# The order of optional blocks at the end of a routed expert layer

## Chip, cores and metric

The kernel runs on one core of one Trainium2 chip. The metric is device time in microseconds, as the median of several runs. All data are float32.

## The reference

A mixing layer (the real part of a Fourier transform along the sequence and along the features) feeds a layer of eight experts. Each of the 19968 rows goes to the one expert with the highest logit.

```
X = np.fft.fft(x, axis=1)              # x: (8, 2496, 256)
X = np.fft.fft(X, axis=2)
x = X.real.reshape(19968, 256)

logits = x @ w_gate                    # (19968, 8)
expert_idx = np.argmax(logits, axis=1)
# ... gate_w: softmax probability of the chosen expert
# ... rows sorted by expert; lo, hi bound the rows of expert e
for e in range(E):
    h = np.maximum(x_sorted[lo:hi] @ w1[e], 0.0)   # 256 -> 1024
    y_sorted[lo:hi] = h @ w2[e]                    # 1024 -> 256
y = gate_w[:, None] * y_sorted[inv_perm]
```

How many rows each expert gets is known only when the kernel runs.

## The kernel before

The eight batches are mixed one after the other. Their rows are scattered into a buffer `Xs` in HBM, grouped by expert. Between the mixing steps, and then alone, the kernel works through a list of blocks. A block has 512, 256 or 128 rows of one expert. Which expert and which rows is read from a table that the kernel computes on the chip; the number of blocks and their order are fixed when the program is built.

The last round has five blocks of 512 rows, seven of 256 rows (numbered 0 to 6), and 21 small blocks of 128 rows (numbered 0 to 20). The first 14 small blocks exist whatever the routing is. Small blocks 14 to 20 are optional: they take up the partly filled ends of the experts, and a routing may need fewer than all of them.

```
    # rounds(), last batch
    k = full(done, BLK)                                   # 7 blocks of BLK = 256 rows
    now.append((BLK, k, False))
    now.append((REST, (NT - used + E * (REST - 1)) // REST, True))   # 21 blocks of REST = 128

SURE = -(-(NT - sum(size * k for now in rounds() for size, k, last in now if not last)) // REST)   # 14

def in_order():
    todo = []
    for b, now in enumerate(rounds()):
        parts = [[(b, size, last, i) for i in range(k)] for size, k, last in now]
        if b == B - 1:
            few, many = parts[-2:]
            sure, more = many[:SURE], many[SURE:]
            k = len(few)
            rest = []
            for i in range(k):
                rest += few[i:i + 1] + sure[len(sure) * i // k:len(sure) * (i + 1) // k][:1]
                rest += more[len(more) * i // k:len(more) * (i + 1) // k]
                rest += sure[len(sure) * i // k:len(sure) * (i + 1) // k][1:]
            parts = parts[:-2] + [rest]
        todo += sum(parts, [])
    return todo
```

A block loads its rows and the two weight matrices of its expert, 1 MiB each. Rows and weights have three buffers each, so a block reuses the buffers of the third block before it. The loads of up to three blocks, the current one included, are asked for in the order of the list, all on one queue:

```
    def fetch_rows(b, size, tab, i):
        ...
        xb = bp.tile([128, BIG // 128, W], F32, tag="xb", name="xb", bufs=3)
        taken(nc.sync.dma_start(out=xb..., in_=Xs[ds(row, size)]...), b)          # L528

    def fetch_weights(tab, i):
        ...
        w1_sb = bp.tile([128, 2, F], F32, tag="w1", name="w1_sb", bufs=3)
        nc.sync.dma_start(out=w1_sb[:], in_=w1[ds(ev, 1)]...)                      # L535
        w2_sb = bp.tile([128, FC, D], F32, tag="w2", name="w2_sb", bufs=3)
        nc.sync.dma_start(out=w2_sb[:], in_=w2[ds(ev, 1)]...)                      # L537
```

Products of an optional block stand in a branch. If the block isn't used, a short product of a bfloat16 tile of ones takes their place. Everything else of an unused block still runs: loads, transposes, the activations, and the scatter of its rows, whose indices lie outside the output.

```
        @contextmanager
        def needed(last, at, o):
            if not last or at < SURE:
                yield
                return
            ...                       # used = number of small blocks that this routing has
            with tc.If(used > at) as has:
                yield
            with has.Else():
                mm(o[:], ones[0:1], bc(ones[0:1], 1, o[0:1].free_size() // 128))
```

A small block, in the order in which TensorE sees it. `turn` is the transpose of the next block's rows; it stands between the two products.

```
            for f in range(FC // m):                         # two rounds for a small block
                ph = pse.tile([128, m, size], F32, tag="ac"[f % 2], name="ph")
                with needed(last, at, ph):
                    ...  mm(ph[:, j], w1_sb[...], xT[:, c, 0:size], c == 0, c == 1)
                ...      # relu into hT, on ScalarE or VectorE
            ...
            for i in range(n):                               # n = 1 for a small block
                xT = next(turned, xT)                        # transposes pt, L576, L577
                py = pse.tile([128, D], F32, tag="bd"[i % 2], name="py")
                with needed(last, at, py):
                    ...  mm(py[:], hT[...], w2_sb[:, f], f == 0, f == FC - 1)
                y = bp.tile([128, D], F32, tag="y", name="y", bufs=6)
                act.activation(y[:], py[:], ACTF.Copy, scale=xb[:, i, D + 1:D + 2])   # L830
                put_row(out, ro[:, i:i + 1], y[:], NT - 1, "out")
```

The blocks of 256 rows use a scheme of seven products in place of eight, in both layers (products a, b, c, d and e in the profile). It needs sums and differences of the weights, which VectorE makes while the block before runs:

```
    class Left:
        def __init__(self, w1_sb):
            ws = bp.tile([128, 3, F // 2], F32, tag="ws", name="ws", bufs=2)
            ...
        def step(self):
            ...
                vec.tensor_tensor(o, p, q, op=op)            # L556: ws <- w_sb, four operations
```

Of the kernel before, what the change touches and what calls it, by code (L numbers as in the profile page):

```python
# [131 lines left out]
def rounds():  # L132

    want = [((256, 2), (128, 4)), ((256, 4),)] + [((512, B),)] * (B - 2)
    plan, used = [], 0

    def full(done, size):
        return max(0, -(-(done - used - E * (size - 1)) // size))  # L140

    for b in range(B):
        done = (b + 1) * S
        now = []
        for size, most in want[b]:
            k = min(full(done, size), most)
            if k:
                now.append((size, k, False))
            used += size * k
        if b == B - 1:  # L150
            k = full(done, BLK)
            used += BLK * k
            now.append((BLK, k, False))
            now.append((REST, (NT - used + E * (REST - 1)) // REST, True))
        plan.append(now)
    return plan
# [6 lines left out]
# [7 lines that stand above are left out]
            few, many = parts[-2:]  # L170
            sure, more = many[:SURE], many[SURE:]
            k = len(few)
            rest = []
            for i in range(k):
                rest += few[i:i + 1] + sure[len(sure) * i // k:len(sure) * (i + 1) // k][:1]
                rest += more[len(more) * i // k:len(more) * (i + 1) // k]
                rest += sure[len(sure) * i // k:len(sure) * (i + 1) // k][1:]
            parts = parts[:-2] + [rest]
        todo += sum(parts, [])
    return todo  # L180

# [33 lines left out]
def kernel(ctx: ExitStack, tc, x, w_gate, w1, w2, out):  # L215
# [687 lines left out]

    tabs, whole = {}, set()
    todo = in_order()
    for _ in first(0):
        pass
# [108 lines left out]
```

## Time and profile before

| | |
|---|---|
| median of three runs | 1347.98 us (1344.14 to 1348.62) |
| span of the profiled execution | 1337.0 us |
| mean granted TensorE clock | 0.979 |
| HBM traffic over the span | 187 GB/s |
| loads of weights | 132, of 1024 KB each |
| scaled tiles y of 128 rows | 129 |

A row of the page's groups has the source line, the engine and the operation, then what it writes and reads, and how often. After the first bar stand busy time in us and mean length in ns, after the second the idle time ahead of it and what ended most of that. In the chain of waits a row has the start in us, the length in us and what it was. PE is TensorE, DVE is VectorE, ACT is ScalarE, POOL is GpSimd, SPq is the sequencer that issues the loads.

A row of a window has the stretch in us and its length, then busy time of PE, PEld (weight loads into the array), DVE, ACT and POOL, each with its number of instructions, then the granted clock, the busy share of the DMA engines and GB/s.

### The profile page before, as it was taken

What the parts mean: (1) busy time and instruction counts of PE and PEld (TensorE: products, weight loads), DVE (VectorE), ACT (ScalarE), POOL (GpSimd) and SP (SyncE); (2) the same over time, 40 slices, a digit from 0 to 9 for tenths busy, and PEclk for the clock granted to TensorE, in tenths of its full rate; (3) what the DMA queues carried; (4) which work ended last, traced back from release to release, by engine and by line L of the source; (5) the groups of instructions that cost most, each with busy time, mean ns of one, the idle gap of its engine ahead of it and who ended that gap; (6) DMA issues with size and microseconds to landing.
All of it is one profiled execution on the core that took longest, in us unless ns stands there. A gap on an engine that the chain in (4) does not pass through costs nothing.

```text
span 1337.0 us, 20538 instructions
## 1 busy us (share of the span) xinstructions
PE 1272.2 (95%) x7231; PEld 1115.2 (83%) x7231; DVE 706.6 (53%) x1772; ACT 396.2 (30%) x942; POOL 359.8 (27%) x355
## 2 busy tenths in 40 slices
PE   6778997999999999999999999999999999999998
PEld 4667985786688888888888888888889999999887
DVE  4554153243356655565356655467478775444453
ACT  1422131131134332442234333342223232222222
POOL 0335214125211521044111531144354221111111
PEclk9869998999999999999999999999999999999999
DMA  8877867535534832455223742234343237777774
GB/s 248 259 260 275 325 221 248 192 102 161 202 109 155 293 132 99 132 199 198 103 103 119 236 160 103 95 134 141 112 144 148 88 110 288 281 281 276 284 284 173
DMA packets 63107, 249.73 MB, mean 187 GB/s; under 512 B 10057, under 2 KB 24883, under 8 KB 43420
## 3 DMA queue, kind: packets, MB, share of 16 engines
q1 hardware_dynamic: 46231, 203.33, 44.3%
q0 software_dynamic: 15888, 42.14, 8.6%
q10 hardware_dynamic: 885, 2.94, 0.7%
q8 instruction: 59, 0.97, 0.3%
q14 instruction: 44, 0.36, 0.1%
HBM read 194.97 MB, written 54.83 MB: 187 GB/s over the span
## 4 chain that ended last, share of the span: by engine, by line
PE 86%; DMA 4%; DVE 3%; issue 3%; another core or an unknown queue 2%; ACT 1%; POOL 0%; SPq 0%; POOLq 0%; ACTq 0%; DVEq 0%
PE py L220 31%; PE ph L220 10%; PE c L220 10%; PE a L220 9%; PE d L220 6%; PE p L220 6%; PE b L220 5%; PE e L220 4%; PE s L220 3%; PE pt L576 3%; DMA w_sb<-in_moe_w_dram 1%; DMA Td<-t 1%; DMA t<-Td 1%; DMA xq<-in_x_dram 1%
## 5 line engine op out<-in xcount | busy, mean ns | idle before, releaser
L220 PE MATMUL py<-w_sb,hT 128*128 128x256 f32 x2016 | 458.8, 381 | 4.0 <-DVE hT L789 4.0
L220 PEld LDWEIGHTS py<-w_sb,hT 128*128 128x128 f32 x2016 | 375.9, 191 | 52.2 <-DVE hT L789 4.8
L235 POOL DMA_INDIRECT out_dram<-y,ro x163 | 161.9, 993 | 794.0 <-ACT y L830 556.2
L235 POOL DMA_INDIRECT Xs<-rows,pi x160 | 161.9, 1012 | 176.4 <-DVE rows L410 52.3
L220 PE MATMUL ph<-xT,w_sb 128*128 128x128 f32 (+2 forms) x992 | 176.4, 333 | 15.7 <-issue 9.9
L830 ACT ACTIVATE y<-py,xb 128x256 f32<-128x256 f32 x129 | 61.1, 474 | 390.6 <-PE py L220 374.8
L220 PEld LDWEIGHTS ph<-xT,w_sb 128*128 128x128 f32 x992 | 137.7, 195 | 43.8 <-issue 26.9
L220 PE MATMUL a<-xT,w_sb 128*128 128x256 f32 (+1 forms) x512 | 118.3, 358 | 4.3 <-DVE xT L577 4.3
L789 DVE TENSOR_SCALAR hT<-ph 128x512 f32<-128x512 f32 x43 | 29.7, 690 | 172.8 <-issue 77.6
L614 DVE TENSOR_TENSOR u<-p,b 128x512 f32<-128x512 f32 x57 | 39.2, 687 | 138.3 <-PE b L220 96.1
L220 PEld LDWEIGHTS a<-xT,w_sb 128*128 128x128 f32 x512 | 89.6, 192 | 15.1 <-DVE xT L577 5.1
L408 DVE COPY lg<-p 128x16 f32<-128x16 f32 x80 | 13.9, 173 | 128.5 <-ACT zs L405 118.8
L577 DVE TENSOR_SCALAR xT<-pt,table 128x512 f32<-128x512 f32 (+1 forms) x94 | 63.3, 673 | 31.2 <-PE pt L576 31.1
L624 ACT ACTIVATE hT<-a 128x512 f32<-128x512 f32 x57 | 34.0, 597 | 153.8 <-PE a L220 134.1
L220 PE MATMUL s<-xq,w 104*112 104x256 f32 (+2 forms) x208 | 63.3, 428 | 14.8 <-DVE xq L297 11.1
L220 PEld LDWEIGHTS p<-table,t 120*128 120x128 f32 x352 | 55.3, 206 | 11.4 <-issue 4.9
L220 PE MATMUL p<-table,t 120*128 120x120 f32 (+1 forms) x352 | 59.9, 294 | 2.8 <-issue 1.4
L791 ACT ACTIVATE hT<-ph 128x512 f32<-128x512 f32 x55 | 32.8, 597 | 98.9 <-PE ph L220 77.1
L220 PE MATMUL p<-table,zz 128*128 128x145 f32 (+1 forms) x320 | 57.6, 304 | 4.6 <-issue 2.7
L220 PE MATMUL c<-xT,ws 128*128 128x256 f32 (+1 forms) x256 | 59.0, 357 | 2.8 <-DVE hT L620 2.8
L220 PEld LDWEIGHTS s<-xq,w 104*112 104x112 f32 x208 | 39.4, 207 | 25.5 <-DVE xq L297 10.1
L220 PE MATMUL b<-xs,ws 128*128 128x256 f32 (+1 forms) x256 | 59.6, 361 | 0.0
(146 smaller groups left out, 1785.0 us busy)
## 6 DMA issues: line engine op xcount, KB each, us to landing
w_sb<-in_moe_w_dram SPq DMA_DIRECT2D x132, 1024.0 KB
xq<-in_x_dram SPq DMA_DIRECT2D x24, 896.0 KB
xb<-Xs SPq DMA_DIRECT2D x28, 516.0 KB
Td<-t SPq DMA_DIRECT2D x18, 448.0 KB
t<-Td SPq DMA_DIRECT2D x8, 768.0 KB
t<-Td SPq DMA_DIRECT2D x8, 640.0 KB
xb<-Xs SPq DMA_DIRECT2D x13, 258.0 KB
xb<-Xs SPq DMA_DIRECT2D x25, 129.0 KB
```

Source lines behind the costliest of these rows:

```text
L220: nc.tensor.matmul(o, lhsT=lhsT, rhs=rhs, start=start, stop=stop, **kw)
L235: return unordered(pool.indirect_dma_start(out=dst, out_offset=bass.IndirectOffsetOnAxis(ap=idx, axis=0), in_=rows, in_offset=None, bounds ...
L408: vec.tensor_copy(lg[:, k:k + 2], p3[:, NY:NY + 2 * E].rearrange("p (m e) -> p m e", m=2))
L576: nc.tensor.transpose(pt[:, c, t], xb[:, 2 * h + t, c * 128:(c + 1) * 128], ident[:])
L577: vec.tensor_scalar(xT[:, :, 256 * h:256 * h + 128 * n], pt[:].rearrange("p c t k -> p c (t k)"), con["alt"][:], None, op0=ALU.mult)
L614: vec.tensor_tensor(u2[:], p1[:], b[:], op=add)
L624: act.activation(h11, a[:], ACTF.Relu)
L789: vec.tensor_scalar(o, ph[:], 0.0, None, op0=ALU.max)
L791: act.activation(o, ph[:], ACTF.Relu)
L830: act.activation(y[:], py[:], ACTF.Copy, scale=xb[:, i, D + 1:D + 2])
```

## The change

Before, the seven optional small blocks are spread: one behind each 256-block and its first sure small block. Now the first four of them stay among the blocks, each between the two sure small blocks of its 256-block as before, and the other three are put behind everything else. A routing that needs few optional blocks then has the unused ones at the end of the list. Loads, products and branches of each block are untouched.

```
             few, many = parts[-2:]
             sure, more = many[:SURE], many[SURE:]
             k = len(few)
+            end = more[(len(more) + 1) // 2:]
+            more = more[:len(more) - len(end)]
             rest = []
             for i in range(k):
                 rest += few[i:i + 1] + sure[len(sure) * i // k:len(sure) * (i + 1) // k][:1]
-                rest += more[len(more) * i // k:len(more) * (i + 1) // k]
+                rest += more[i:i + 1]
                 rest += sure[len(sure) * i // k:len(sure) * (i + 1) // k][1:]
-            parts = parts[:-2] + [rest]
+            parts = parts[:-2] + [rest + end]
         todo += sum(parts, [])
     return todo
```

The end of the list, with B for a block of 256 rows, s for a sure small block and o for an optional one:

```
before  ... B4 s8 o18 s9  B5 s10 o19 s11  B6 s12 o20 s13
after   ... B4 s8 s9  B5 s10 s11  B6 s12 s13  o18 o19 o20
```

Up to B4 and s8 both lists are the same.

More of the change, by code (lines that the diff above doesn't have):

```diff
@@ L172, in in_order @@
             k = len(few)
+            end = more[(len(more) + 1) // 2:]
+            more = more[:len(more) - len(end)]
             rest = []
@@ L175, in in_order @@
                 rest += few[i:i + 1] + sure[len(sure) * i // k:len(sure) * (i + 1) // k][:1]
-                rest += more[len(more) * i // k:len(more) * (i + 1) // k]
+                rest += more[i:i + 1]
                 rest += sure[len(sure) * i // k:len(sure) * (i + 1) // k][1:]
-            parts = parts[:-2] + [rest]
+            parts = parts[:-2] + [rest + end]
         todo += sum(parts, [])
```

## The prediction

> **What bounds the kernel now.** I read the page first, then the chain of waits and one-microsecond windows for the last 230 us, because the change only moves blocks there. The page:
>
> ```profile
> PE 1272.2 (95%) x7231; PEld 1115.2 (83%) x7231; DVE 706.6 (53%) x1772; ACT 396.2 (30%) x942; POOL 359.8 (27%) x355
> PE 86%; DMA 4%; DVE 3%; issue 3%; another core or an unknown queue 2%; ACT 1%; POOL 0%; SPq 0%; POOLq 0%; ACTq 0%; DVEq 0%
> L220 PE MATMUL py<-w_sb,hT 128*128 128x256 f32 x2016 | 458.8, 381 | 4.0 <-DVE hT L789 4.0
> L830 ACT ACTIVATE y<-py,xb 128x256 f32<-128x256 f32 x129 | 61.1, 474 | 390.6 <-PE py L220 374.8
> ```
>
> TensorE carries 86% of the chain. The last two rows also say how many optional blocks are absent on these inputs: a 128-row tile of py takes 16 records (the chain shows x16 per small block), so 2016 / 16 = 126 tiles were multiplied, yet 129 were scaled into y. Three tiles had no product. Py from the stand-in operand ones runs at 1257.7, 1291.7 and 1323.9 us, so these are small blocks 18, 19 and 20, behind small blocks 8, 10 and 12. They are exactly the three that the change moves.
>
> How the last stage runs when nothing is absent is in the chain, at the first product of 256-blocks 2, 3 and 4 (columns: start, length, what):
>
> ```profile
> 1167.53 0.89 PE a L220 x8
> ...
> 1202.21 0.89 PE a L220 x8
> ...
> 1236.88 0.89 PE a L220 x8
> ```
>
> One 256-block with three present small blocks takes 34.67 us twice running, and all of it is TensorE in the chain. So weights, four pairs of 1 MiB per 34.67 us, don't bound it. From 1236.88 on it is different:
>
> ```profile
> 1253.40 3.47 PE py L220 x16
> 1256.89 0.48 ACT y L830
> 1257.39 0.34 SPq L528
> ...
> 1258.55 7.08 DMA w_sb<-in_moe_w_dram
> 1265.65 0.70 DVE ws L556
> ...
> 1268.27 0.67 DVE xT L577
> 1268.94 0.04 issue
> 1268.99 1.76 PE a L220 x8
> 1270.75 1.71 PE b L220 x8
> 1272.45 1.11 PE d L220 x8
> 1273.56 0.89 PE c L220 x8
> ```
>
> Here small block 8 ends, absent block 18 follows, and 256-block 5 needs the weight buffer that small block 8 has just released (three buffers, so block k uses that of block k-3). The absent block passes in under 2 us, small block 9 in 7.4 us, and the load (7.08 us), the four DVE operations on it and the turn of xT come out later than that. TensorE waits, then also runs at a reduced clock:
>
> ```profile
> 1268.00:1269.00 1.00, 0.01 (x1) 0.01 (x1) 0.97 (x3) 0.00 (x0) 0.52 (x1) 1.00 1.03 421
> 1269.00:1270.00 1.00, 1.00 (x6) 1.00 (x7) 0.93 (x4) 0.00 (x0) 0.00 (x0) 0.69 1.09 459
> 1270.00:1271.00 1.00, 1.00 (x7) 1.00 (x7) 0.96 (x3) 0.22 (x1) 0.00 (x0) 0.50 0.94 387
> ```
>
> (Last three columns: granted clock, DMA share, GB/s.) An absent block therefore costs more than its own few instructions: it is too short to hide the load that it sits in front of.
>
> **What the Trainium skill says.** "Trace Analysis", section Identifying Performance Opportunities, says that the same gap repeating on the engine that should be saturated can mean too few buffers. The trace agrees: the wait appears behind both absent blocks that have a 256-block two places later. "TensorE: Matmul & The Clock Gate", Part 1, says that an idle window of about 3.4 us, free-running, halves the clock. Here the idle stretch is 2.6 us after a nearly idle microsecond at 1258, and 0.50 is granted at 1270; the second such gap, 1.7 us at 1300.4, brought no drop. So direction agrees and the threshold is not settled here. "DMA: Bandwidth & Descriptors", Anatomy of one DMA, gives about 2.0 us plus bytes / 436 GB/s, fitted on another issue path. For the 2.2 MB of rows and weights of a small block that is an estimate of 7.1 us; the trace has 8.9 us, from the issue of the rows at 1316.57 to the last busy DMA window, ending near 1325.45.
>
> **The change, removed part.** The undisturbed length without any optional block is 34.67 minus one small block. In the chain a small block is 3.57 (ph) + 0.22 (pt) + 3.46 (py) = 7.25 us; so 34.67 - 7.25 = 27.42 us. The three groups before, from starts of the first product a:
> - 256-block 4 to 5: 1268.99 - 1236.88 = 32.11, excess 4.69 (about 1.8 for the absent block itself, 2.6 for the wait).
> - 256-block 5 to 6: 1302.06 - 1268.99 = 33.07, excess 5.65 (1.9 from the slow clock on three products of 0.89, 1.8 absent block, 1.7 wait).
> - 256-block 6 to the last y at 1332.14: 30.08. Undisturbed it is 27.42 less 0.22, since no 256-block follows and two transposes fewer are needed: 27.20. Excess 2.88 (1.8 absent block, about 1.0 for late ws operands).
> Sum 13.2 us. After the change the same three buffers suffice: each 256-block takes the buffer of the 256-block before it, which is free two small blocks (14.7 us) ahead, against a load of about 9 us. I expect all 13.2 to go, and the last present y to start at 1332.14 - 13.2 = 1318.9.
>
> **The change, added part.** Before, the span ended 4.9 us after the last y started (1337.0 - 1332.14). Now three absent blocks follow. Their instructions take about 1.8 us each, or 5.4. But absent block 20 loads its rows and both weight matrices although nothing multiplies them, and their buffers are those of small block 13, the last present one. So that load cannot start before its y is scaled. From the same pattern before: y starts, 0.48 later it is done, rows are issued, and 8.9 us later the DMA engines are quiet: 9.4 us. The program ends only when each transfer has landed; for the completion and the closing barrier I take 1.5 us, a choice somewhat below the 2 us that lie between the last busy DMA window (1334 to 1335) and the end at 1337.0 before. That makes 10.9 us. Beside it lies the compute path: rows landed about 2.5 us after y, transposes, the stand-ins of two blocks, y and the scatter: about 7 us to the scatter and 2 to 3 to the end, so 9 to 10, hidden under the load. In the built program the stand-ins wait for no weight transfer; only the multiplied branch does. So the tail grows from 4.9 to 10.9: plus 6.0.
>
> Elsewhere nothing moves: 1671 TensorE instructions are listed for both, and the order before small block 8 is the same. Sum: -13.2 + 6.0 = -7.2 us. 1347.98 - 7.2 = 1340.8 us, or 0.5%.
>
> **Rivals.** (1) *The tail takes it all back.* If only the stand-ins' 3 x 1.8 = 5.4 us leave the middle and the waits remain in another form, -5.4 + 6.0 = +0.6: 1348.6. For it: DMA is 77 to 79% busy in the windows from 1120 to 1280, so the load may simply bind later. Against: the undisturbed groups carry four pairs of weights in 34.67 us, a denser load than three pairs in 27.4, without one wait, and DMA stands at 0 GB/s from 1312 to 1315. (2) *The tail is longer:* the load of absent block 19 is still running when that of 20 begins, and stand-ins might queue behind weights; 14 us of tail would leave -4: 1344. (3) *The tail is hidden further:* if the load finishes at the measured bandwidth peak and the closing is short, about 8.5 us after y, the gain is 9.6: 1338.4. (4) *TensorE, with no gaps, loses clock.* Against it: granted clock 1.00 through 1120 to 1240 us at 100% busy. I give it little.
>
> **Range and chances.** The mechanism spans -10 to +1 around -7.2; the three runs before span 4.5 us (1344.14 to 1348.62), which blurs a median by some 2 us. Together I take 1335.5 to 1346.0. 2% would be 27 us, more than the whole tail and all three waits together, so within 2% is 0.98, and 0.01 each side.
>
> **What would show it.** Right: products a of 256-blocks 4, 5 and 6 are 27.4 us apart, no chain piece of w_sb between them, the clock at 1.00, last y of a present block near 1319, then TensorE almost idle, DMA at about 400 GB/s for 5 to 6 us after it, and the end 11 us after. Wrong in the middle: groups of 29 us or more, with DVE ws still waiting for DMA. Wrong at the end: the last chain pieces are ACT and POOL rather than the weights, or the end comes over 13 us after the last present y.

## The result, and the profile after

The changed kernel takes 1336.3 us (1332.64 to 1337.62) against 1347.07 us (1344.14 to 1348.62) for the one before: ratio 0.9918, 95% interval 0.9892 to 0.9945. Forecast were 1340.8 us and a range of 1335.5 to 1346.0. Measured again in two later sets of runs, the ratio was 0.9948 (0.9933 to 0.9962) and 0.9951 (0.9933 to 0.9969), which is 6.9 and 6.6 us. The forecast gain of 7.2 us lies in both later intervals, and just outside the first, which begins at 7.4 us.

The page of the changed kernel, in the rows that answer to those of before. (The change adds two lines to the source, so L220 is now L222 and L830 is L832.)

```profile
PE 1269.9 (95%) x7231; PEld 1113.9 (83%) x7231; DVE 708.2 (53%) x1772; ACT 396.7 (30%) x942; POOL 359.1 (27%) x355
PE 69%; issue 19%; POOL 3%; DVE 3%; DMA 2%; another core or an unknown queue 2%; ACT 1%; POOLq 0%; ACTq 0%; DVEq 0%; SPq 0%
L222 PE MATMUL py<-w_sb,hT 128*128 128x256 f32 x2016 | 458.5, 381 | 3.9 <-DVE hT L791 3.9
L832 ACT ACTIVATE y<-py,xb 128x256 f32<-128x256 f32 x129 | 61.2, 474 | 396.4 <-PE py L222 381.4
```

The work is the same: equal numbers of instructions, 2016 records of py, 129 tiles y. The second row misleads. TensorE has not fallen from 86% to 69% of what bounds the kernel. The chain of this trace is followed back along GpSimd's own queue, where long stretches are only called issue; in a second trace of the same kernel it stays with TensorE, at 88%. For this kernel the timeline and the windows tell more.

The middle first: 256-block 5 in the timeline of after (start, length, then the instruction; in brackets the idle time ahead of it and what ended that).

```profile
1253.29 0.34 SPq L530 DMA_DIRECT2D xb<-Xs  x1
1254.74 0.05 SPq L537 DMA_DIRECT2D w_sb<-in_moe_w_dram  x1
...
1263.28 0.69 DVE L558 TENSOR_TENSOR ws<-w_sb 128x512 f32<-128x512 f32 x1 [6.03 <-DMA w_sb<-in_moe_w_dram]
...
1265.82 0.74 DVE L579 TENSOR_SCALAR xT<-pt,table 128x512 f32<-128x512 f32 x1
...
1267.05 1.05 PE L222 MATMUL a<-xT,w_sb 128*128 128x128 f32 x8
```

Its load is now asked for when 256-block 4 ends. DVE still waits for it, 6 us long, but TensorE does not: two present small blocks run meanwhile, and product a has no bracket. The reserve is thin. The load lands 10.0 us after its rows were asked for, DVE needs 3.3 us more until xT is ready at 1266.56, and a starts 0.5 us later.

Now the end, first in the timeline of after. The last present block scales its y at 1322.31.

```profile
1322.31 0.47 ACT L832 ACTIVATE y<-py,xb 128x256 f32<-128x256 f32 x1 [4.82 <-PE py L222]
...
1322.81 0.34 SPq L530 DMA_DIRECT2D xb<-Xs  x1
...
1326.56 0.41 PE L578 MATMUL pt<-table,xb 128*128 128x128 f32 x2 [2.41 <-DMA xb<-Xs]
...
1328.83 0.47 ACT L832 ACTIVATE y<-py,xb 128x256 f32<-128x256 f32 x1 [0.46 <-issue]
1329.58 0.97 POOL L237 DMA_INDIRECT out_dram<-y,ro  x1 [0.64 <-ACT y L832]
```

The rows of absent block 20 are asked for 0.50 us after that y starts and let TensorE go on 3.75 us later. Its y starts at 1328.83, its scatter at 1329.58; the end comes 4.9 us after that. In the windows the DMA share and GB/s are the last two columns:

```profile
1324.00:1325.00 1.00, 0.15 (x1) 0.00 (x0) 0.73 (x2) 0.44 (x1) 0.70 (x2) 1.00 0.93 286
...
1330.00:1331.00 1.00, 0.00 (x0) 0.00 (x0) 0.00 (x0) 0.00 (x0) 0.55 (x1) 0.50 0.74 295
1331.00:1332.00 1.00, 0.00 (x0) 0.00 (x0) 0.00 (x0) 0.00 (x0) 0.00 (x0) 0.50 0.07 9
```

So the DMA engines work for the absent blocks until about 1331, with TensorE nearly idle.

Executions differ by 2 to 3 us before 256-block 4 even starts, where both kernels have the same instructions (the changed kernel reached it 2.9 us later in the first pair of traces, 2.1 us in the second). I therefore cut the traces at its first product. What follows is called the stage; a group runs from one 256-block to the next. All numbers below are us, from the starts of product a of 256-blocks 4, 5 and 6 (B4, B5, B6), the last present y, and the end.

| kernel | B4 to B5 | B5 to B6 | B6 to last present y | y to end | sum | ratio to before (interval) |
|---|---|---|---|---|---|---|
| before | 32.27 | 33.07 | 30.08 | 4.86 | 100.28 | 1 |
| before, again | 32.18 | 32.77 | 30.08 | 4.85 | 99.88 | 0.9996 (0.9981 to 1.0011) |
| after | 27.44 | 27.84 | 27.42 | 12.19 | 94.89 | 0.9918 (0.9892 to 0.9945) |
| after, again | 27.44 | 27.43 | 27.48 | 12.69 | 95.04 | 0.9948 (0.9933 to 0.9962) |
| after, third | 27.43 | 27.72 | 27.41 | 12.24 | 94.80 | 0.9951 (0.9933 to 0.9969) |
| without 18, 19, 20 | 27.43 | 27.44 | 27.20 | 4.57 | 86.64 | 0.9898 (0.9882 to 0.9913) |
| optional block ahead of both | 30.80 | 30.96 | 30.02 | 4.85 | 96.63 | 0.9957 (0.9940 to 0.9974) |
| middle, no weights loaded | 31.48 | 32.94 | 30.08 | 4.89 | 99.39 | 1.0017 (0.9999 to 1.0035) |
| middle, loads in a branch | 30.80 | 32.10 | 30.11 | 4.89 | 97.90 | 1.0011 (0.9995 to 1.0026) |
| middle, no weights, asked earlier | 29.49 | 29.49 | 29.25 | 5.00 | 93.23 | 0.9923 (0.9895 to 0.9950) |
| block 20 alone at the end | 32.50 | 33.56 | 29.15 | 5.82 | 101.03 | 0.9979 (0.9959 to 1.0000) |
| end, no weights loaded | 27.43 | 27.44 | 27.41 | 9.52 | 91.80 | 0.9938 (0.9920 to 0.9956) |
| end, loads in a branch | 27.43 | 27.44 | 27.41 | 9.56 | 91.84 | 0.9934 (0.9911 to 0.9957) |
| end, loads in a branch, again | 27.44 | 27.92 | 27.41 | 9.75 | 92.52 | 0.9926 (0.9894 to 0.9957) |

Ratios are to runs of the kernel before on the same chip, whose median was 1347, 1318, 1319 or 1343 us. From the traces the change is worth 5.2 us (three traces of after, mean 94.91, against two of before, mean 100.08): 12.7 won in the middle, 7.5 lost at the end. Each trace is a single execution. In this table trace and timing differ by nearly 6 us in the first measurement of after and by up to 3.8 us in the others, in either direction.

### The profile page after: what moved, and what is told of

Same layout as the page of the kernel before. It is cut to its first block, busy times and chain, and to the rows that moved or that the text cites. A ratio compares the mean times of both kernels' runs of the same rounds, so it can differ in the third digit from the quotient of the medians.

```text
span 1334.5 us, 20538 instructions
## 1 busy us (share of the span) xinstructions
PE 1269.9 (95%) x7231; PEld 1113.9 (83%) x7231; DVE 708.2 (53%) x1772; ACT 396.7 (30%) x942; POOL 359.1 (27%) x355
## 4 chain that ended last, share of the span: by engine, by line
PE 69%; issue 19%; POOL 3%; DVE 3%; DMA 2%; another core or an unknown queue 2%; ACT 1%; POOLq 0%; ACTq 0%; DVEq 0%; SPq 0%
PE py L222 27%; PE p L222 7%; PE c L222 7%; PE a L222 6%; PE ph L222 6%; PE d L222 4%; PE s L222 3%; PE b L222 3%; POOL out_dram L237 3%; PE e L222 3%; PE pt L578 2%; DMA Td<-t 1%; DMA t<-Td 1%; DVE s L775 1%
## 5 line engine op out<-in xcount | busy, mean ns | idle before, releaser
L222 PE MATMUL py<-w_sb,hT 128*128 128x256 f32 x2016 | 458.5, 381 | 3.9 <-DVE hT L791 3.9
L222 PEld LDWEIGHTS py<-w_sb,hT 128*128 128x128 f32 x2016 | 375.6, 191 | 51.9 <-DVE hT L791 4.7
L222 PE MATMUL ph<-xT,w_sb 128*128 128x128 f32 (+2 forms) x992 | 177.5, 335 | 15.8 <-issue 10.4
L832 ACT ACTIVATE y<-py,xb 128x256 f32<-128x256 f32 x129 | 61.2, 474 | 396.4 <-PE py L222 381.4
L222 PEld LDWEIGHTS ph<-xT,w_sb 128*128 128x128 f32 x992 | 138.5, 195 | 44.3 <-issue 29.2
L222 PE MATMUL a<-xT,w_sb 128*128 128x256 f32 (+1 forms) x512 | 117.4, 356 | 0.0
L222 PEld LDWEIGHTS a<-xT,w_sb 128*128 128x128 f32 x512 | 89.3, 190 | 10.1
L222 PE MATMUL s<-xq,w 104*112 104x256 f32 (+2 forms) x208 | 63.3, 429 | 13.6 <-DVE xq L299 11.3
L222 PEld LDWEIGHTS p<-table,t 120*128 120x128 f32 x352 | 55.1, 206 | 11.0 <-issue 3.6
L222 PE MATMUL p<-table,zz 128*128 128x145 f32 (+1 forms) x320 | 57.6, 304 | 5.2 <-issue 2.7
L222 PE MATMUL p<-table,t 120*128 120x120 f32 (+1 forms) x352 | 59.4, 293 | 2.6 <-ACT t L374 1.1
L222 PE MATMUL c<-xT,ws 128*128 128x256 f32 (+1 forms) x256 | 59.0, 357 | 1.2 <-DVE hT L622 0.6
L222 PEld LDWEIGHTS s<-xq,w 104*112 104x112 f32 x208 | 39.4, 207 | 24.3 <-DVE xq L299 10.1
L222 PE MATMUL d<-xT,w_sb 128*128 128x256 f32 (+1 forms) x256 | 58.7, 356 | 0.0
```

Of the source, the lines that this page charges most:

```text
L222: nc.tensor.matmul(o, lhsT=lhsT, rhs=rhs, start=start, stop=stop, **kw)
```

## Experiments

**Both kernels again.** No edit.

> The kernel before once more, unchanged. From the first product of 256-block 4 to the end it took 100.3 us in the first trace. Theory A (the whole gain lies in the last stage): this stage is 100 to 101 us again, and the ratio to before is 1.000. Rival B (the last stage of before is often worse than in its first trace, because the slow clock after the two waits falls differently each time): the stage is 2 to 6 us longer than 100.3 in this trace, which would explain why the runs differ by 11 us and the stage in the traces by only 5.4.

The last stage took 99.88 us and the ratio was 0.9996. Rival B gets no support: in this second trace the stage of before is not worse than in the first.

> The changed kernel once more, unchanged. Theory A: 0.9945 to 0.996 of before (5.4 to 7.4 us less), the stage from 256-block 4 to the end near 94.9 us as in its first trace. Rival C (the program as a whole got another 5 us from the part before 256-block 4, where both have the same instructions): 0.992, and the first product of 256-block 4 earlier than in before by about 5 us.

> The changed kernel a third time, beside the two kernels that it is compared with: 0.993 to 0.996 of before, stage 95 us, tail 12 to 13 us.

Ratios 0.9948 and 0.9951, stages 95.04 and 94.80, as theory A has it, at the upper side of its gain. Rival C (0.992) lies outside both intervals, and product a of 256-block 4 came at 1219.06 in after, against 1216.92 in before on the same chip: no gain hides there. The 0.9918 of the first measurement was not met again.

**Without the three absent blocks.** What do they cost at either place?

```
-            parts = parts[:-2] + [rest + end]
+            parts = parts[:-2] + [rest]
```

> The changed order with optional blocks 18, 19 and 20 left out altogether (this routing has no rows for them; another routing could). It shows what the three cost at either place. Theory A: groups 27.4, 27.8 and 27.3 us as after, the end 4.9 us behind the last y, so the stage takes 87.6 us: 12.7 less than before and 7.3 less than after; ratio to before 0.990. Rival D (the wait in the middle comes from the rate of DMA, not from the absent blocks): groups stay near 29 us or more, ratio above 0.994.

The stage took 86.64 us, within 1 us of the forecast. So the three cost 13.4 us in the middle and 8.3 us at the end. Rival D falls here.

**The optional block ahead of both small blocks.** All 21 are loaded.

```
-                rest += few[i:i + 1] + sure[len(sure) * i // k:len(sure) * (i + 1) // k][:1]
-                rest += more[len(more) * i // k:len(more) * (i + 1) // k]
-                rest += sure[len(sure) * i // k:len(sure) * (i + 1) // k][1:]
+                rest += few[i:i + 1] + more[len(more) * i // k:len(more) * (i + 1) // k]
+                rest += sure[len(sure) * i // k:len(sure) * (i + 1) // k]
```

> Order before, but in each group the optional block stands ahead of both sure small blocks, directly behind the 256-block. All 21 blocks are loaded. The next 256-block then takes the buffer of the optional block, free two whole small blocks (14.7 us) ahead. Theory A (an absent block costs much only because it is the short cover of a 256-block's load): the waits go, only the 1.8 us of each absent block stay: groups of 29.2, 29.2 and 29.0, end 4.9 later, stage 92.3 us, so 8 less than before and 2.6 less than after; ratio 0.994. Rival D (DMA rate): four loads in a group take 32 us or more wherever the absent one stands; stage 100 us, ratio 1.000. Rival E: the second small block behind the absent one now waits for its load (cover 9.2 us), groups of 30.5 to 32, stage 96 us.

Groups of 30.80 and 30.96: neither 29.2 nor 32. (The ratio, 0.9957 with 0.9940 at the lower end, just allows theory A as well; it is the groups that speak against it.) The 256-block's buffer is indeed free early, but so is another. In the timeline of this kernel:

```profile
1233.30 0.34 SPq L534 DMA_DIRECT2D w_sb<-in_moe_w_dram  x1
...
1235.05 0.34 SPq L527 DMA_DIRECT2D xb<-Xs  x1
1236.20 0.71 SPq L534 DMA_DIRECT2D w_sb<-in_moe_w_dram  x1
...
1245.94 0.69 DVE L555 TENSOR_TENSOR ws<-w_sb 128x512 f32<-128x512 f32 x1 [7.78 <-DMA w_sb<-in_moe_w_dram]
...
1249.27 1.16 PE L219 MATMUL a<-xT,w_sb 128*128 128x128 f32 x8 [0.98 <-DVE xT L576]
```

The absent block passes so quickly that two loads are asked for within 3 us. The second, for the 256-block, lands 9.7 us after its issue, and TensorE waits 0.98 us. The windows show 385 to 464 GB/s in every microsecond from 1236 to 1246, so I read this as D in small: not the mean rate of DMA but two loads at once. No run tested that reading alone. Rival E's size was right, but the block that waits is the 256-block.

**In the middle, absent blocks without weights.** Order before; blocks 18 to 20 share the weight tiles of the block ahead of them, so nothing is loaded for them. That leaves out their weights, which this routing doesn't use.

```
+                    if last and at >= MOST - 3:
+                        got.append(shared[0])
+                    else:
                         got.append(fetch_weights(tabs[b, size, last], at))
+                    shared[:] = got[-1:]
```

> Order before, but blocks 18, 19 and 20 load no weights and take no weight buffers: in the program they share those of the block ahead (a routing that used them would get wrong rows; this one doesn't). Rows, stand-ins, activations and scatters stay. Theory A2 (the wait in the middle is the load of the next 256-block made late by the absent block's own load and by the buffer that it turns over): both waits go, each absent block costs its 1.6 to 1.8 us alone. Groups 29.2, 29.2, 29.0, tail 4.9, stage from 256-block 4 to the end 92.3 us against 100 before; ratio 0.994. Rival F (an absent block is itself what holds TensorE up, through its branches and the rows that it loads): groups stay at 31 us or more, ratio 0.998 or above.

Nothing gained: 1.0017, groups of 31.48 and 32.94. Theory A2 falls, at least as it was put, and these are the sizes that rival F named. From the timeline of this kernel:

```profile
1237.58 0.47 ACT L835 ACTIVATE y<-py,xb 128x256 f32<-128x256 f32 x1 [4.80 <-PE py L220]
...
1238.08 0.34 SPq L528 DMA_DIRECT2D xb<-Xs  x1
...
1239.20 0.34 SPq L535 DMA_DIRECT2D w_sb<-in_moe_w_dram  x1
...
1245.55 0.69 DVE L556 TENSOR_TENSOR ws<-w_sb 128x512 f32<-128x512 f32 x1 [6.23 <-DMA w_sb<-in_moe_w_dram]
...
1248.89 1.16 PE L220 MATMUL a<-xT,w_sb 128*128 128x128 f32 x8 [1.82 <-DVE xT L577]
```

By the order in which the buffers turn, the weights of the 256-block had a free one here long before 1239. But they stand on one queue behind its rows, and the rows still rotate through three buffers: their load waits for the y of small block 8 (1237.58, 0.47 long) and is issued at 1238.08. The weights follow 1.1 us later. On this reading a wait on one buffer holds up everything behind it on the queue; the run that asks earlier, below, tests it against rival F.

**In the middle, loads in a branch.** Written to be right for every routing (only this one was run): an absent block loads 8 columns of each matrix.

```
+            with tc.If(some > i) as has:
+                nc.sync.dma_start(out=w1_sb[:], ...)
+                nc.sync.dma_start(out=w2_sb[:], ...)
+            with has.Else():
+                nc.sync.dma_start(out=w1_sb[:, 0, 0:8], in_=w1[0, :, 0, 0:8])
+                nc.sync.dma_start(out=w2_sb[:, 0, 0:8], in_=w2[0, :, 0, 0:8])
```

> Order before, and the loads of the weights of every optional block (14 to 20) stand in a branch on the queue that issues them: an absent block loads 8 columns of each matrix instead of 1 MiB. Right for every routing. The buffers are still turned over by the absent blocks. If the waits come from the bytes of the absent block's load, they go as in the kernel without loads: stage 92.5 to 93.5 us, ratio 0.994 to 0.995. If they come from the buffer alone (the 256-block still takes the buffer of the small block ahead of the absent one, free only 9.2 us earlier), the first operation on ws still comes 6 to 7 us behind the release and the stage stays at 96 us or more, ratio 0.997 or above.

The stage is 97.90 us, and the times show no gain (1.0011). TensorE still waits, 1.15 us and 1.62 us at the starts of 256-blocks 5 and 6, which fits if the moment of asking is what counts. That the trace shows 2 us less than before and the times do not is left open.

**In the middle, no weights, and asked for earlier.** As the kernel without weights in the middle, and:

```
-        xb = bp.tile([128, BIG // 128, W], F32, tag="xb", name="xb", bufs=3)
+        xb = bp.tile([128, BIG // 128, W], F32, tag="xb", name="xb", bufs=4)
-        def fetch_some(k, most=3):
+        def fetch_some(k, most=4):
-                y = bp.tile([128, D], F32, tag="y", name="y", bufs=6)
+                y = bp.tile([128, D], F32, tag="y", name="y", bufs=3)
```

> The kernel before with 18, 19 and 20 loading no weights (as in the run that showed no gain in the middle), and in addition four row buffers in place of three and loads asked for up to four blocks ahead; y has three buffers in place of six, to make room. A 256-block behind an absent block can then ask for rows and weights when the 256-block before it ends, 16 us ahead. Theory A3 (the wait is when the load is asked for: the 256-block's rows wait for the buffer of the small block ahead of the absent one, and its weights stand behind those rows in one queue): the waits on ws go, groups 29.2, 29.2, 29.0, tail 4.9, stage 92.3 us, ratio 0.993 to 0.995. Rival F (the absent block itself, its branches and its rows, holds TensorE up): groups stay at 31 us or more, stage 98 us or more, ratio 0.999 or above.

The waits go: 29.49, 29.49, 29.25, ratio 0.9923. The timeline has the rows of the 256-block asked for before the absent block, directly when 256-block 4 has scaled its last rows:

```profile
1254.15 0.34 SPq L528 DMA_DIRECT2D xb<-Xs  x1
...
1263.41 0.69 DVE L556 TENSOR_TENSOR ws<-w_sb 128x512 f32<-128x512 f32 x1 [1.03 <-DMA w_sb<-in_moe_w_dram]
...
1269.96 1.05 PE L220 MATMUL a<-xT,w_sb 128*128 128x128 f32 x8
```

What remains of an absent block is 29.49 - 27.43 = 2.06 us, its own passing. Rival F falls. So where absent blocks load no weights the wait is settled: it comes from when the next load is asked for (the fourth row buffer and the deeper asking were not taken apart). For the kernel before, whose absent blocks do load them, it is inferred that the excess is this passing plus the wait and its consequences; earlier asking with those loads in place, which would need four buffers of weights, was not tried.

**Block 20 alone at the end.**

```
-            end = more[(len(more) + 1) // 2:]
+            end = more[-1:]
```

> The changed order for block 20 alone: it goes to the very end, 18 and 19 stay in the middle. If the parts add up, groups are 32.1, 33.0 (both with their waits), the last group 27.2 (2.9 less), the tail that of one absent block behind the last present one: its load is asked for when the block two before the last ends, so it is over in time, and the tail is 1.8 + 4.9 = 6.7 us; stage 99.0 us, 1 less than before, ratio 0.999. If every block at the end costs the long tail, it is 11 us or more, the stage 103 us and the ratio 1.002 or above.

The tail is 5.82 us: one absent block at the end is cheap, since its load was asked for earlier. But the last group took 29.15 us, not 27.2, so the parts did not add up. TensorE waited before 256-block 6:

```profile
1306.73 1.41 PE L222 MATMUL a<-xT,w_sb 128*128 128x128 f32 x8 [2.18 <-DVE xT L579]
```

Then its clock was 0.50 for a while. From this a to the first ph behind the 256-block it took 14.46 us, against 12.72 undisturbed; these 1.74 us are the whole excess of the last group over the 27.41 of after. In before the pause there was 1.69 us, the clock stayed at 1.00, and the same stretch took 13.56 us. So of the 2.9 us that I had booked to block 20, about 0.8 come from the late start of 256-block 6, which is block 19's doing, and 2.05 are block 20's own (29.25 - 27.20, from the run that asks earlier and the one without the three). In time the ratio 0.9979 is 2.8 us less than before, while the trace is 1 us longer; that stays open.

**At the end, without weights.** The changed order with the same sharing.

> Changed order, with the same sharing: 18, 19 and 20 at the end, without loads of weights. It takes the tail of 12.2 to 12.7 us apart. Theory W (the unneeded 2 MiB loads make the tail long, directly and by delaying the rows of block 20 and the last scatter): rows of block 20 land 2.2 us after their issue and not 3.7, the scatter's end comes 3 us behind its issue, tail 9 to 10 us, stage 92.3 us, ratio 0.993 to 0.9925. Rival G (the chain of rows, transposes, stand-ins and scatter sets the tail whatever DMA does): tail above 11.5 us, ratio 0.995.

The tail shrinks from 12.2 to 12.7 us to 9.52. Its end in the timeline:

```profile
1300.48 0.34 SPq L530 DMA_DIRECT2D xb<-Xs  x1
...
1302.65 0.66 PE L578 MATMUL pt<-table,xb 128*128 128x128 f32 x2 [0.82 <-DVE hT L796]
...
1305.69 0.97 POOL L237 DMA_INDIRECT out_dram<-y,ro  x1 [0.30 <-issue]
```

TensorE turns the rows of block 20 2.2 us after their issue and not 3.75, and now waits for DVE there and no longer for the rows. From the last scatter to the end (1309.5) it takes 3.8 us and not 4.9. Theory W holds. Still 9.5 us remain that no load of weights explains: rows, transposes, stand-ins, y and scatter.

**At the end, loads in a branch.** The same branch, in the changed order.

> Changed order with the loads in the same branch. Right for every routing. Middle as after (27.4, 27.4, 27.4). By theory W the tail shrinks to 9 to 10.5 us: stage 92 to 93 us, ratio 0.9925 to 0.9935, 2 to 3 us less than after. By rival G it stays at the time of after.

> The changed order with the optional blocks' weights loaded in a branch, again, beside the changed kernel: stage 91.8 us as in its first trace, 3 us less than the changed kernel; ratio to before 0.9915 to 0.9935.

The tails are 9.56 and 9.75 us, the stages 91.84 and 92.52: 2.4 to 3.1 us less than the mean of after. The last present y and that of block 20, in the timeline of the first:

```profile
1298.24 0.47 ACT L847 ACTIVATE y<-py,xb 128x256 f32<-128x256 f32 x1 [4.82 <-PE py L222]
...
1303.13 0.47 ACT L847 ACTIVATE y<-py,xb 128x256 f32<-128x256 f32 x1
```

The y of block 20 starts 4.9 us after that of the last present block, against 6.5 in after. In time the ratios are 0.9934 and 0.9926 against 0.9948 and 0.9951. Their intervals overlap, so that this kernel beats the changed one is shown by its tail in the traces, not by the times alone.

## Why the prediction was right

By its steps:

- *Which blocks are absent, and an undisturbed group of 27.42 us.* Right: 27.43 to 27.84 in three traces of after. (The prediction's count of 1671 TensorE instructions stands in no profile; the pages list 7231 products for both kernels.)
- *13.2 us go from the middle.* Right in sum. Leaving the three blocks out takes 13.4 us off the stage, 13.2 of it ahead of the last y; after itself loses 12.7. The starts were read from the chain, which shows a piece only from where the one before it ends: 1236.88 for product a of 256-block 4. The timeline has it at 1236.72, so the first group was taken 0.16 too short. The split by block was poorer: about 0.8 us of what I gave to block 20 belong to block 19, and an absent block's own passing is 2.05 us where I took 1.8.
- *Why TensorE waits: the short block is the only cover, and the buffer is free too late.* The cover was right. The buffer was named too narrowly. Weights with a free buffer still waited, behind rows whose buffer was not free, and only earlier asking for both removed the wait (1.82 us at 256-block 5 without it, none with it).
- *Three buffers suffice afterwards.* Right, with less to spare than "14.7 us against about 9" sounds: 10.0 us for the load, 3.3 for DVE, 0.5 left. Two of the traces lose 0.3 to 0.4 us between B5 and B6; in the first trace of after, product c of 256-block 5 waits 0.33 us for DVE.
- *The tail grows from 4.9 to 10.9.* The mis-sized term: it is 12.2 to 12.7. The load itself was nearly right, its last busy window ends at 1331, 8.7 us after y against the 9.4 forecast. What failed is "hidden under the load" for the compute path at 9 to 10 us. The prediction's own sign for this, a chain that ends in POOL and not in the weights, is there in after:

```profile
1327.97 0.97 POOL out_dram L237
1328.94 0.40 issue
1329.34 1.20 POOLq L1013
```

(The chain of before ends on POOL's queue too, so the sign alone says little; the lengths decide.) The last scatter began 7.3 to 7.7 us after y, near the 7 forecast, although the rows of block 20 let TensorE go on only 4.1 to 4.6 us after y and not 2.5. From there to the end I had put 2 to 3 us; it took 4.9 to 5.0. The trace of before had 4.1 for the same stretch (1332.89 to 1337.0), and I should have used it. Without the loads the scatter begins 5.7 us after y and the end comes 3.8 us later, so the two paths aren't beside each other: the load slows the compute path.
- *Sum.* -13.2 + 6.0 = -7.2 was forecast. The traces have -12.7 + 7.5 = -5.2, the three timings -10.8, -6.9 and -6.6. Both terms missed in the same direction, by 0.5 and 1.5 us. That the timings lie nearer to 7.2 than the traces do is not explained by any step; so close a hit of the number is partly luck.
- *Rivals.* That the tail takes all back fell: the middle gave 12.7, not 5.4. (The DMA share quoted for it is 76 to 79%.) The longer tail (2) came closest to what happened, though what was late were the rows of block 20 and the end of the last scatter. A loss of clock (4) did not occur: 1.00 in every window from 1262 to 1296.

## What to carry to other kernels

A block that turns out empty costs not only its own instructions. It is a hole in the cover for the next load, and where everything is asked for on one queue, as here, the load behind it starts no earlier than the slowest buffer ahead of it. Moving empty blocks to the end removes the hole, but there nothing covers the last of their loads; so leave those out (a branch on the issuing queue took 2.6 to 2.8 us off the mean tail of 12.4), and check a tail path by what runs on the same DMA engines, not beside an idle machine.

## What the runs showed of the hardware that was not expected

TensorE's clock fell after pauses shorter than the roughly 3.4 us that the Trainium skill gives ("TensorE: Matmul & The Clock Gate", Part 1); here the measurement decides. In the kernels with a wait at the start of a 256-block it fell to 0.50 for some 3 us after pauses of 2.62, 2.47, 2.83 and 2.18 us, and stayed at full speed after 1.90, 1.82, 1.69, 1.62 and 1.38 us and after shorter ones. That is no threshold, though. Earlier in the same executions a pause of 3.00 us at the same place of the program was followed by a drop in one trace and by none in another; of eight traces with this pause (2.98 to 3.00 us) three show the drop. The second run of before, then the second of after (in a window, the third column from the end is the granted clock):

```profile
967.32 1.12 PE L576 MATMUL pt<-table,xb 128*128 128x128 f32 x4 [3.00 <-DVE xT L577]
968.00:969.00 1.00, 1.00 (x7) 1.00 (x6) 0.53 (x1) 0.00 (x0) 0.00 (x0) 0.50 0.00 0
```

```profile
970.94 0.66 PE L578 MATMUL pt<-table,xb 128*128 128x128 f32 x4 [3.00 <-DVE xT L579]
972.00:973.00 1.00, 1.00 (x12) 1.00 (x10) 0.39 (x1) 0.00 (x0) 0.00 (x0) 1.00 0.08 16
```

In the run that asks earlier the clock stayed at 1.00 even after a pause of 3.58 us, at 342.38. So the length of the pause alone does not decide; what else does is not shown here, and a shorter wait may or may not cost clock.

Where the clock falls, it can do so about a microsecond after work has begun again. In the second run of before the pause of 2.47 us ends at 1249.10:

```profile
1249.00:1250.00 1.00, 0.90 (x8) 0.90 (x9) 0.90 (x5) 0.00 (x0) 0.00 (x0) 1.00 1.00 401
1250.00:1251.00 1.00, 1.00 (x9) 1.00 (x8) 0.96 (x4) 0.59 (x1) 0.00 (x0) 0.68 0.97 401
1251.00:1252.00 1.00, 1.00 (x7) 1.00 (x6) 0.97 (x2) 0.00 (x0) 0.00 (x0) 0.50 0.96 400
```

The block loses 1.7 us: its second product a starts 5.31 us after the first, against 3.57 undisturbed. Here a wait of 2.5 us so costs over 4.
